# Banded attention into a gated feed-forward on one core: the softmax's guard, its division, two scalar loads and the last chunk's output projections are arranged anew

## The chip, the core and the metric

The kernel runs on one core of a Trainium2 chip. Its engines run side by side and wait for each other by semaphores: TensorE (PE in the profile) multiplies matrices into PSUM, VectorE (DVE), ScalarE (ACT) and GpSimd (POOL) do the elementwise work, and SyncE (SP) issues most DMAs. The metric is the device time of one execution in microseconds, lower is better.

## What is computed

```python
scores = q @ k.T / sqrt(64)                       # 4 batches, 8 heads, 768 positions
keep   = (pos_k < n_sink) | ((0 <= rel) & (rel < window))     # 4 sinks, window 128
scores = where(keep, scores, -1e9); scores -= scores.max(-1)
a = exp(scores); a = a / (a.sum(-1) + 1e-9)
x = (a @ v), heads side by side                   # 3072 x 512
out = (sigmoid(x @ w_gate) * (x @ w_val)) @ w_out # 512 -> 1536 -> 512
```

The weights come as 64-bit floats, so the kernel decodes each into a high and a low 32-bit part. Every product of the feed-forward is made as three products of such parts, which is why TensorE has three matmuls where one would be thought of.

## The kernel before

**The order of the work** is decided when the kernel is built. Each piece of work is handed to a planner (`Plan.op`, line 264) with a priority, the tiles that it reads and writes, and one or more *ways*: an engine, a guessed time in ns and the function that issues it. `Plan.run` (line 288) plays the guessed times forward and, whenever an engine is guessed to be free, gives it the waiting piece with the lowest priority whose buffers are free. The order that comes out is then issued as it stands, engine by engine, and each engine works through its own list in order. So a changed guess or a changed piece can move instructions anywhere in the program. Where PE has nothing to do early on, the planner puts in filler matmuls on the identity (`warm`, line 649; `m<-ident` in the profile), whose results nobody reads.

**Attention** (`attend`, line 692) runs in 96 units: 4 batches x 3 pairs of query tiles x 8 heads. A unit is a chain. PE makes the scores of both tiles `t` (`a<-qkT` in the first 16 units, `a<-kh,qs` later); DVE applies the masks `am` and writes the scores into `P` with the row's extreme in `negm_all` (`top`); ACT takes the exponential in place and adds up each row into `rs` (`exp`, line 751, with the instruction ACTIVATION_READ_ACCUMULATOR behind it). Then `guard` (line 764, on POOL or DVE) adds 1e-9 to both sums, DVE takes the reciprocal (line 771), each tile's 128 band columns are multiplied by it (line 773; ACT, POOL or DVE), and `sink_weights` (line 792, on DVE or POOL) multiplies the 4 sink columns of both tiles into their place in `psk`, where those of all 8 heads are gathered. PE turns `P` (`a<-ident,P`), ACT copies it to `wt`, POOL cuts it to the two triangles (the two affine selects of `split`), and PE multiplies it with `v`. `P` and `rs` have two buffers each, so at most two units are between their scores and their transposes. After 8 heads, `join` (line 928) adds the sinks' part and leaves x in the tiles `XH` and `XL`.

**The feed-forward** (`feed`, line 1061, and `feed_part`, line 1089) runs over 8 chunks `ci` of 2 to 4 token tiles (`MT`, line 25) and in each over 12 blocks `f` of 128 hidden columns. A block has 12 gate and 12 value matmuls into two PSUM tiles `m`, a tanh on ACT (`th`), the product on DVE, a rounded high part `gh` (ACT or DVE), the rest `gl` (POOL or DVE, `rest`, line 520), and then the output projections `down` (line 1145): three matmuls for each token tile into `o`, which read `gh`, `gl`, `woh` and `wol`. PE's priority for a block's `down` is half a block behind its gate matmuls. `th`, `gh` and `gl` have two buffers each.

**Around them**: `decode` (line 995) turns 36 weight tiles into parts during the first 200 us or so, shared out over ACT, DVE and POOL (`wst`, `w`, `wgh`, `wgl`, `wvl`, `wlo` ...). The two scalars `n_sink` and `window` are loaded by the first two DMAs of SP's queue (line 571), the masks wait for them. The last lines (1183 to 1203) count whether the general path is needed: a matmul `count`, a cast, a reduction `total`, which every engine then reads before it branches.

Of the kernel before, what the change touches and what calls it, by code (L numbers as in the profile page):

```python
# [433 lines left out]
def kernel(  # L434
# [136 lines left out]
    for i, s in enumerate((n_sink, window)):  # L571
        dma(
            SCALP, 56.0, lambda i=i, s=s: Q.dma_start(
                out=nums()[:, 2 * i : 2 * i + 2],
                in_=s.bitcast(I32).rearrange("(o x) -> o x", o=1).broadcast_to([128, 2]),
            ), w=[(nums, i)],
# [67 lines left out]

    MS = [ps.tile([128, 512], F32, name=f"m{i}") for i in range(BUFS["m"])]
# [46 lines left out]
    def attend(u, b, h, t0, T, XR, XS, PSK):  # L692
# [35 lines left out]
        rs = tile([128, 4], F32, "rs", BUFS["P"])  # L728
        for t in range(T):
# [21 lines left out]
            def exp(t=t):  # L751
                A.activation(
                    out=P()[:, t], in_=P()[:, t], func=AF.Exp, bias=negm_all[:, u, t : t + 1],
                    scale=-1.0, accum_out=rs()[:, t : t + 1],
                )
# [6 lines left out]
            plan.op(u, [("A", 460, exp)], [], [(P, t), (rs, t)])  # L762

        def guard(E):
            return lambda: E.tensor_scalar(
                out=rs()[:, 0:T], in0=rs()[:, 0:T], scalar1=1.0e-9, scalar2=None, op0=ALU.add
            )

        plan.op(u, [("G", 400, guard(G)), ("V", 250, guard(V))], [], [rs])
        plan.op(  # L770
            u, [("V", 120, lambda: V.reciprocal(out=rs()[:, 0:T], in_=rs()[:, 0:T]))], [], [rs]
        )
        for t in range(T):
            plan.op(
                u, [
                    ("V", 390, lambda t=t: V.tensor_scalar(
                        out=P()[:, t, 0:128], in0=P()[:, t, 0:128], scalar1=rs()[:, t : t + 1],
                        scalar2=None, op0=ALU.mult,
                    )),
                    ("A", 320, lambda t=t: A.mul(  # L780
                        out=P()[:, t, 0:128], in_=P()[:, t, 0:128], mul=rs()[:, t : t + 1]
                    )),
                    ("G", 450, lambda t=t: G.tensor_scalar(
                        out=P()[:, t, 0:128], in0=P()[:, t, 0:128], scalar1=rs()[:, t : t + 1],
                        scalar2=None, op0=ALU.mult,
                    )),
                ][::-1],
                [rs], [(P, t)],
            )


        def sink_weights(E):
            return lambda: E.tensor_tensor(
                out=psk()[:, 0:T, h], in0=P()[:, 0:T, 128:KW],
# [458 lines left out]
```

## Time and profile before

| | |
|---|---|
| device time, three runs | 796.38, 798.26, 807.41 us; median 798.26 us |
| the profiled execution, its own time | 798.38 us |
| its span in the trace | 796.7 us (1.7 us lie around it) |
| PE busy | 773.8 us, 97% of the span |
| DVE, ACT, POOL busy | 513.4, 403.2 and 437.5 us (64%, 51%, 55%) |
| mean granted PE clock | 0.992 of full speed |

The busy times are of the whole span, but the stages differ: DVE, ACT and POOL work mainly in the first 400 us and little in the last 200, PE nearly all the time. Matmuls are pipelined and their ends are modelled, so the time of one is read from the starts of neighbours; a busy PE can still hold filler matmuls. A wait is credited to the instruction that came last.

### The profile page before, as it was taken

The page shows a single profiled execution, that of the slowest core. Times are in us where ns is not written, and L with a number is a line of the kernel's source. Part 1 is how long each engine was busy: PE and PEld are TensorE (multiplying, and loading weights), DVE is VectorE, ACT ScalarE, POOL GpSimd, SP SyncE. Part 2 cuts the span into 40 slices and gives each one's busy share as a digit, 9 for nine tenths or more (in the row PEclk, how much of TensorE's full clock was granted, in tenths as well). Part 3 has the DMA queues.
Part 4 walks back from the last instruction along what each step waited for, and adds up shares of the span by engine and source line. Part 5 has one row for each costly group of instructions (what it writes and reads, how often), then busy time and mean ns, then how long its engine had stood idle before and what let it go on. Part 6 is the DMA issues. An engine that isn't in the chain of part 4 may idle for free. (4 is left out here: it accounts for less than half of the span.)

```text
span 796.7 us, 14763 instructions
## 1 busy us (share of the span) xinstructions
PE 773.8 (97%) x4540; PEld 702.8 (88%) x4540; DVE 513.4 (64%) x1550; ACT 403.2 (51%) x1190; POOL 437.5 (55%) x602
## 2 busy tenths in 40 slices
PE   7999999999999999999999999999999999999996
PEld 5677798878999999998999999999999999999995
DVE  5787798998799988899871388885861331111110
ACT  4786777766767767676640256664740210011001
POOL 3676798887667778668761267673751221111211
PEclk8999999999999999999999999999999999999999
DMA  5667777763645544444441235343311121113111
GB/s 162 198 190 207 191 213 253 231 201 115 192 126 151 149 107 122 119 116 112 142 113 40 57 104 133 104 129 111 92 45 42 41 79 40 40 40 92 39 42 57
DMA packets 98421, 94.33 MB, mean 118 GB/s; under 512 B 43168, under 2 KB 77984, under 8 KB 98336
## 3 DMA queue, kind: packets, MB, share of 16 engines
q1 hardware_dynamic: 98336, 93.32, 41.1%
q8 instruction: 38, 0.62, 0.3%
q14 instruction: 47, 0.39, 0.1%
HBM read 83.85 MB, written 9.44 MB: 117 GB/s over the span
## 5 line engine op out<-in xcount | busy, mean ns | idle before, releaser
L488 DVE SCALAR_TENSOR_TENSOR th<-th,m 128x384 f32<-128x384 f32 (+1 forms) x108 | 54.6, 505 | 184.3 <-PE m L488 182.9
L488 POOL TENSOR_TENSOR gl<-th,gh 128x384 fp32r<-128x384 f32 (+1 forms) x65 | 65.5, 1008 | 195.4 <-DVE gh L488 183.0
L488 ACT ACTIVATE th<-m 128x384 f32<-128x384 f32 (+1 forms) x108 | 49.1, 454 | 209.4 <-PE m L488 207.5
L488 POOL TENSOR_SCALAR_AFFINE_SELECT wt<-wt 128x512 fp32r<-128x512 f32 (+3 forms) x192 | 121.5, 633 | 42.6 <-DVE wt L488 24.2
L488 PE MATMUL m<-XH,wvh 128*128 128x384 f32 (+1 forms) x432 | 140.1, 324 | 0.4 <-ACT th L488 0.4
L488 PE MATMUL m<-XH,wgh 128*128 128x384 f32 (+1 forms) x432 | 140.3, 325 | 0.0
L488 PE MATMUL m<-XH,wvl 128*128 128x384 f32 (+1 forms) x432 | 137.7, 319 | 0.0
L488 PE MATMUL m<-XL,wvh 128*128 128x384 f32 (+1 forms) x432 | 137.6, 319 | 0.0
L488 PE MATMUL m<-XH,wgl 128*128 128x384 f32 (+1 forms) x432 | 137.5, 318 | 0.0
L488 PE MATMUL m<-XL,wgh 128*128 128x384 f32 (+1 forms) x432 | 137.3, 318 | 0.0
L488 PE MATMUL o<-woh,gh 128*128 128x512 f32 x276 | 113.0, 409 | 1.0 <-DVE total L1201 1.0
L488 PE MATMUL o<-woh,gl 128*128 128x512 f32 x276 | 109.5, 397 | 2.2 <-DVE gl L488 1.6
L488 PE MATMUL o<-wol,gh 128*128 128x512 f32 x276 | 108.8, 394 | 2.5 <-DMA wol<-wol_d 2.5
L488 ACT ACTIVATE P<-P,negm_all 128x132 f32<-128x132 f32 x192 | 77.2, 402 | 30.5 <-DVE negm_all L488 27.0
L488 PEld LDWEIGHTS m<-XH,wvh 128*128 128x128 f32 x432 | 81.7, 189 | 3.3 <-ACT th L488 0.6
L488 PEld LDWEIGHTS m<-XH,wgh 128*128 128x128 f32 x432 | 81.4, 189 | 2.1 <-issue 0.2
L488 PEld LDWEIGHTS m<-XL,wvh 128*128 128x128 f32 x432 | 81.8, 189 | 1.5
L488 PEld LDWEIGHTS m<-XL,wgh 128*128 128x128 f32 x432 | 81.5, 189 | 1.6
L488 PEld LDWEIGHTS m<-XH,wvl 128*128 128x128 f32 x432 | 81.7, 189 | 0.0
L488 PEld LDWEIGHTS m<-XH,wgl 128*128 128x128 f32 x432 | 81.3, 188 | 0.0
L488 PEld LDWEIGHTS o<-woh,gl 128*128 128x128 f32 x276 | 52.0, 188 | 16.6 <-DVE gl L488 3.5
L488 DVE CUSTOM_DVE_ANT_0 P<-a,am 128x132 f32<-128x132 f32 x192 | 56.2, 294 | 11.9 <-PE a L488 2.9
(115 smaller groups left out, 1619.5 us busy)
## 6 DMA issues: line engine op xcount, KB each, us to landing
wol<-wol_d SPq DMA_DIRECT2D x108, 256.0 KB, 2.7
qkT<-in_k_dram SPq DMA_DIRECT2D x120, 99.0 KB, 2.6
qkT<-in_q_dram SPq DMA_DIRECT2D x176, 64.0 KB, 2.4
wst<-in_moe_w_gate_dram SPq DMA_DIRECT2D x12, 512.0 KB, 4.3
wst<-in_moe_w_val_dram SPq DMA_DIRECT2D x12, 512.0 KB, 4.3
wst<-in_moe_w_out_dram SPq DMA_DIRECT2D x12, 512.0 KB, 4.2
vraw<-in_v_dram SPq DMA_DIRECT2D x64, 96.0 KB, 2.3
out_dram<-w SPq DMA_DIRECT2D x23, 256.0 KB, 2.5
```

What stands on the lines that cost most here:

```text
L488: return lambda *a, **kw: tc.keep_in_program_order(op(*a, **kw))
```

## The change

- The row sums go into the first column of a constant tile `sums` of [128, 2, 2], two buffers, all filled with 1e-9 once at the start by POOL. The exponential overwrites only column 0 of each pair, so summing the pair adds the guard: one DVE `tensor_reduce`, followed at once on DVE by the reciprocal, both in one piece of the plan.
- The division of both tiles over all 132 columns is one piece with three ways: one POOL `tensor_tensor` against the broadcast reciprocals, two ACT multiplications in a row, or one DVE `tensor_tensor`. The sink columns are divided with it, so `psk` gets a plain copy (POOL or ACT) afterwards.
- The loads of the two scalars are issued by ACT's queue in place of SP's.
- The planner's guess for POOL's byte step of `decode` is 560 in place of 1000 ns.
- In the last chunk the `down` of block `f` gets a priority 1.4 blocks behind its gate matmuls, and the last block's `gl` is made on DVE only.

```diff
-        dma(
-            SCALP, 56.0, lambda i=i, s=s: Q.dma_start(
+        plan.op(
+            SCALP, [("A", 460, lambda i=i, s=s: A.dma_start(
...
+    SUMS = [const.tile([128, 2, 2], F32, name=f"sums{i}") for i in range(BUFS["P"])]
+    for x in SUMS:
+        nc.gpsimd.memset(x, 1.0e-9)
...
-        rs = tile([128, 4], F32, "rs", BUFS["P"])
+        sums = Tile(SUMS, None, F32, "sums", BUFS["P"])
+        rs = tile([128, T], F32, "rs", BUFS["P"])
...
-                    scale=-1.0, accum_out=rs()[:, t : t + 1],
+                    scale=-1.0, accum_out=sums()[:, t, 0:1],
...
-        plan.op(u, [("G", 400, guard(G)), ("V", 250, guard(V))], [], [rs])
-        plan.op(
-            u, [("V", 120, lambda: V.reciprocal(out=rs()[:, 0:T], in_=rs()[:, 0:T]))], [], [rs]
-        )
...
+        def guard():
+            V.tensor_reduce(out=rs(), in_=sums()[:, 0:T], axis=AX.X, op=ALU.add)
+            V.reciprocal(out=rs(), in_=rs())
+
+        plan.op(u, [("V", 320, guard)], [sums], [rs])
+        def norm(E):
+            return lambda: E.tensor_tensor(
+                out=P(), in0=P(), in1=rs().unsqueeze(2).to_broadcast([128, T, KW]), op=ALU.mult
+            )
+        def norm_each():
+            for t in range(T):
+                A.mul(out=P()[:, t], in_=P()[:, t], mul=rs()[:, t : t + 1])
...
-            u, [("V", 110, sink_weights(V)), ("G", 400, sink_weights(G))], [rs, (P, T)], [(psk, h)]
+            u, [("G", 800, norm(G)), ("A", T * 350, norm_each), ("V", 380, norm(V))], [rs], [P]
+        )
+        gather = lambda: psk()[:, 0:T, h]
...
+                ("G", 230, lambda: G.tensor_copy(out=gather(), in_=P()[:, :, 128:KW])),
+                ("A", 250, lambda: A.copy(out=gather(), in_=P()[:, :, 128:KW])),
...
-                ("G", 1000.0, lambda: G.tensor_scalar(out=flat(), in0=by(3), **two)),
+                ("G", 560.0, lambda: G.tensor_scalar(out=flat(), in0=by(3), **two)),
...
+        last = ci == len(MT) - 1
...
-        rest(pr, W, gl, th, gh, [th, gh], [gl])
+        rest(pr, W, gl, th, gh, [th, gh], [gl], last and f == NF - 1)
...
-                pe + 0.5 / NF, [("PE", 3 * mac(DO), down)], [gh, gl, woh, wol], [O[j]]
+                pe + (1.4 if last else 0.5) / NF, [("PE", 3 * mac(DO), down)], [gh, gl, woh, wol], [O[j]]
```

What the planner makes of it, counted over the whole order of the issued program: of the 96 units' divisions 70 go to ACT as pairs (140 instructions), 17 to POOL, 9 to DVE; before, the 192 were 136 on ACT, 45 on POOL and 11 on DVE. The copies into `psk` are 65 on ACT and 31 on POOL; before, 80 multiplications on DVE and 16 on POOL. The 96 reductions are all on DVE; the guards were 43 on DVE and 53 on POOL. `gh` is made on ACT 94 times (before 54) and on DVE 14 times (before 54). PE's work is the same but for 72 filler pieces where there were 69.

**The end of PE's list.** First the last value matmuls of block 11 before (`wvh_151`, `wvl_152`), the `count`, and the first output projections of block 11 (`gh_10014`); the output projections of block 10 stand ahead of these value matmuls.

```order
L488 MATMUL m_90<-XH,wvh_151 128x384
L488 MATMUL m_90<-XL,wvh_151 128x384
L488 MATMUL m_90<-XH,wvl_152 128x384
L1197 MATMUL count<-bad,one 1x4
L488 MATMUL o_9564<-woh_153,gh_10014 128x512
L488 MATMUL o_9564<-wol_9982,gh_10014 128x512
L488 MATMUL o_9564<-woh_153,gl_10016 128x512
```

And of the change, from the last value matmul of block 11 on: the nine projections of block 10 (`gh_9950`) now stand here, those of block 11 (`gh_9992`) behind them, and `count` behind those.

```order
L488 MATMUL m_95<-XH,wvl_156 128x384
L488 MATMUL o_9562<-woh_152,gh_9950 128x512
L488 MATMUL o_9562<-wol_9921,gh_9950 128x512
L488 MATMUL o_9562<-woh_152,gl_9955 128x512
L488 MATMUL o_9567<-woh_152,gh_9950 128x512
L488 MATMUL o_9567<-wol_9921,gh_9950 128x512
L488 MATMUL o_9567<-woh_152,gl_9955 128x512
L488 MATMUL o_9573<-woh_152,gh_9950 128x512
L488 MATMUL o_9573<-wol_9921,gh_9950 128x512
L488 MATMUL o_9573<-woh_152,gl_9955 128x512
L488 MATMUL o_9562<-woh_157,gh_9992 128x512
L488 MATMUL o_9562<-wol_9963,gh_9992 128x512
```

So between the last value matmul and the first projection that needs its result there are now nine matmuls in place of `count` alone.

**The start of ACT's list**, before: the sinks' cast `vsp`, the exponentials of unit 0 (`P_215`) and unit 1 (`P_230`), two steps of weight decoding (`w`), and unit 0's divisions.

```order
L488 ACT_TABLE_LOAD
L488 CAST vsp<-w_190 96x512
L488 ACTIVATE P_215,rs_218<-P_215,negm_all 128x132 x2
L488 ACTIVATE P_230,rs_234<-P_230,negm_all 128x132
L488 ACTIVATE w_241<-wst_205 128x512
L488 ACTIVATE w_248<-wst_209 128x512
L488 ACTIVATE P_215<-P_215,rs_218 128x128 x2
```

And of the change, where unit 0 is `P_223` and unit 1 `P_233`:

```order
L488 DMA nums_160<-in_n_sink_dram 128x2
L488 DMA nums_160<-in_window_dram 128x2
L488 ACT_TABLE_LOAD
L488 CAST vsp<-w_183 96x512
L488 ACTIVATE P_223,sums_90<-P_223,negm_all 128x132
L488 ACTIVATE w_235<-wst_200 128x512
L488 ACTIVATE P_223,sums_90<-P_223,negm_all 128x132
L488 ACTIVATE P_233,sums_91<-P_233,negm_all 128x132
L488 ACTIVATE w_247<-wst_204 128x512
L488 ACTIVATE P_223<-P_223,rs_249 128x132 x2
L488 ACTIVATE P_233,sums_91<-P_233,negm_all 128x132
L488 COPY psk_264<-P_223 128x2x4
```

The two loads lead the list, a decoding step (`w_235`) has come between unit 0's two exponentials, and the copy into `psk` follows the division on the same engine.

**DVE's list in the first units**, before: the guard (TENSOR_SCALAR on `rs`), the reciprocal, and the multiplications of one unit, with the masks of the next (ISA) between them.

```order
L488 TENSOR_SCALAR rs0_286<-rs0_286 128x2
L488 CAST wvh0_96<-w20_248 128x512
L488 RECIPROCAL rs0_286<-rs0_286 128x2
L488 ISA P1_321,negm_all_80<-a0_308,am0_86 128x132
L488 ISA negm_all_80 128x1
L488 TENSOR_TENSOR psk0_255<-P0_276,rs0_286 128x2x4
L488 TENSOR_SCALAR P0_276<-P0_276,rs0_286 128x128
```

And of the change, the unit behind it:

```order
L488 TENSOR_REDUCE rs1_360<-sums1_91 128x2
L488 RECIPROCAL rs1_360<-rs1_360 128x2
L488 ISA P0_366,negm_all_80<-a2_345,am0_86 128x132
L488 ISA negm_all_80 128x1
L488 COPY_PREDICATED a0_348<-tri_89,a0_348 128x128
L488 ISA P0_366,negm_all_80<-a0_348,am1_87 128x132
```

Reduction and reciprocal follow each other, and the multiplications of the sink columns are gone from this list.

## Rows read from the trace of the kernel before

**Rows 1.** The busy time of each engine in stretches of the span. Columns: the stretch and its length in us; then the busy time, with the number of instructions in brackets, of PE, PE's weight loads, DVE, ACT and POOL; then the granted PE clock, the DMA share and GB/s.

```profile
0.00:50.00 50.00, 43.18 (x227) 31.52 (x228) 35.37 (x130) 32.08 (x93) 29.11 (x52) 0.93 0.61 181
50.00:100.00 50.00, 47.87 (x300) 39.10 (x299) 39.42 (x114) 36.54 (x107) 34.19 (x45) 0.97 0.69 198
100.00:150.00 50.00, 48.28 (x339) 44.77 (x339) 46.36 (x103) 38.33 (x100) 45.84 (x48) 1.00 0.77 235
150.00:200.00 50.00, 46.32 (x306) 39.84 (x305) 45.86 (x103) 33.74 (x92) 39.70 (x46) 1.00 0.55 167
200.00:250.00 50.00, 50.00 (x361) 46.73 (x359) 44.22 (x152) 35.50 (x118) 32.98 (x53) 1.00 0.58 161
```

**Rows 2.** The filler matmuls of the first 200 us (count, busy us, mean ns, and idle time of PE ahead of them), and the first gate matmuls of the feed-forward (in the stretch from 40 to 60 us: min/median/max ns, first and last start).

```profile
L488 PE MATMUL m<-ident 128*128 128x128 f32 x138 | 24.8, 320 | 1.6 <-POOL ident masks.py:199 1.4
...
L488 PE MATMUL m<-XH,wgh x9: 278/282/386, 48.7 to 60.0; 128*128 128x256 f32 x9
```

**Rows 3.** The end of the span as a timeline: start in us, duration in us, engine, line, operation, count; in brackets the idle time ahead and what ended it.

```profile
786.05 0.34 PE L488 MATMUL m<-XH,wvl 128*128 128x384 f32 x1
...
786.32 0.19 PE L1197 MATMUL count<-bad,one 128*1 128x4 f32 x2
786.49 0.56 DVE L488 SCALAR_TENSOR_TENSOR th<-th,m 128x384 f32<-128x384 f32 x1 [7.46 <-PE m L488]
...
787.08 0.36 DVE L488 CAST gh<-th 128x384 fp32r<-128x384 f32 x1
...
787.61 1.00 POOL L488 TENSOR_TENSOR gl<-th,gh 128x384 fp32r<-128x384 f32 x1 [7.38 <-DVE total L1201]
...
788.67 0.50 PE L488 MATMUL o<-woh,gl 128*128 128x512 f32 x1 [0.44 <-POOLq L1204]
...
789.94 0.39 PE L488 MATMUL o<-wol,gh 128*128 128x512 f32 x1
...
790.17 0.39 PE L488 MATMUL o<-woh,gl 128*128 128x512 f32 x1
...
790.59 0.60 ACT L488 ACTIVATE qkT<-o 128x512 f32<-128x512 f32 x1
```

**Rows 4.** Groups of instructions over the whole span, forms apart: the operations that the change takes out or rewrites (count, then busy us, mean ns of one, then idle time ahead).

```profile
L488 DVE TENSOR_SCALAR rs<-rs 128x2 f32<-128x2 f32 x43 | 21.4, 497 | 3.6 <-ACT P L488 3.4
...
L488 DVE RECIPROCAL rs<-rs 128x2 f32<-128x2 f32 x96 | 15.0, 157 | 4.1 <-POOL rs L488 3.2
...
L488 DVE TENSOR_TENSOR psk<-P,rs 128x8 f32<-128x8 f32 x80 | 30.4, 379 | 0.5
...
L488 ACT ACTIVATE P<-P,rs 128x128 f32<-128x128 f32 x136 | 50.1, 396 | 22.3 <-DVE rs L488 20.9 <-DVE bad L1187 0.8
...
L488 POOL TENSOR_SCALAR P<-P,rs 128x128 f32<-128x128 f32 x45 | 31.6, 701 | 10.8 <-DVE rs L488 8.4 <-DVE psk L488 1.2 <-ACT wst L488 1.0
...
L488 POOL TENSOR_TENSOR psk<-P,rs 128x8 f32<-128x8 f32 x16 | 3.8, 238 | 1.7 <-DVE rs L488 1.7
```

**Rows 5.** The same groups on DVE between 100 and 200 us alone.

```profile
L488 DVE TENSOR_TENSOR psk<-P,rs 128x8 f32<-128x8 f32 x8 | 6.7, 839 | 0.0
...
L488 DVE RECIPROCAL rs<-rs 128x2 f32<-128x2 f32 x11 | 1.7, 152 | 0.0
...
L488 DVE TENSOR_SCALAR rs<-rs 128x2 f32<-128x2 f32 x2 | 1.2, 600 | 0.0
```

**Rows 6.** DVE's reciprocals, one for each unit: those up to 48.7 us, and those up to 200 us.

```profile
L488 DVE RECIPROCAL rs<-rs 128x2 f32<-128x2 f32 x9 | 1.4, 160 | 0.9 <-POOL rs L488 0.8
...
L488 DVE RECIPROCAL rs<-rs 128x2 f32<-128x2 f32 x29 | 4.5, 156 | 0.9 <-POOL rs L488 0.8
```

**Rows 7.** Groups over the whole span that are nearest to what the change adds.

```profile
L488 POOL TENSOR_TENSOR kl<-qkT,kh 128x264 fp32r<-128x264 f32 x10 | 8.2, 815 | 0.6
...
L488 ACT ACTIVATION_READ_ACCUMULATOR P<-P,negm_all 128x1 f32 x192 | 36.2, 189 | 0.0
...
L488 ACT CAST vhl<-vraw 128x128 fp32r<-128x128 f32 x7 | 2.1, 299 | 3.2 <-PE a L488 3.2
...
L488 ACT CAST gh<-th 128x384 fp32r<-128x384 f32 x23 | 11.8, 513 | 4.0 <-DVE th L488 3.6
```

**Rows 8.** The start of the span as a timeline (columns as in rows 3; SPq is SyncE's DMA queue): the scalars' first load, the first load behind them, the scalars' arrival, the sinks' cast, the first decoding step on ACT, and unit 0's transposes.

```profile
0.80 0.40 SPq L488 DMA_DIRECT2D nums<-in_n_sink_dram  x1
...
1.72 0.56 SPq L488 DMA_DIRECT2D qkT<-in_k_dram  x1
...
4.70 0.24 DVE L488 CAST nums<-nums 128x2 f32<-128x2 uint32 x2 [2.15 <-DMA nums<-in_window_dram]
...
8.05 0.62 ACT L488 CAST vsp<-w 96x512 fp32r<-96x512 f32 x1 [5.98 <-DMA w<-in_v_sink_dram]
...
11.13 0.70 ACT L488 ACTIVATE w<-wst 128x512 f32<-128x512 f32 x1 [1.28 <-DMA wst<-in_moe_w_gate_dram]
...
13.55 0.77 PE L488 MATMUL a<-ident,P 128*128 128x128 f32 x2 [4.05 <-ACT P L488]
```

**Rows 9.** Unit 1 in the timeline: the last row sum is read out, POOL's guard, DVE's reciprocal.

```profile
13.99 0.19 ACT L488 ACTIVATION_READ_ACCUMULATOR P<-P,negm_all 128x1 f32 x1
...
15.69 0.21 POOL L488 TENSOR_SCALAR rs<-rs 128x2 f32<-128x2 f32 x1
...
15.94 0.17 DVE L488 RECIPROCAL rs<-rs 128x2 f32<-128x2 f32 x1 [0.45 <-POOL rs L488]
```

More of the change, by code (lines that the diff above doesn't have):

```diff
@@ L571 @@
     for i, s in enumerate((n_sink, window)):
-        dma(
-            SCALP, 56.0, lambda i=i, s=s: Q.dma_start(
+        plan.op(
+            SCALP, [("A", 460, lambda i=i, s=s: A.dma_start(
                 out=nums()[:, 2 * i : 2 * i + 2],
                 in_=s.bitcast(I32).rearrange("(o x) -> o x", o=1).broadcast_to([128, 2]),
-            ), w=[(nums, i)],
+            ))], w=[(nums, i)], dma=56.0,
         )
@@ L761, in attend @@
             )
[L762 to L766, printed above, removed]
-            )
-        plan.op(u, [("G", 400, guard(G)), ("V", 250, guard(V))], [], [rs])
+            plan.op(u, [("A", 460, exp)], [], [(P, t), (sums, t)])
+        def guard():
+            V.tensor_reduce(out=rs(), in_=sums()[:, 0:T], axis=AX.X, op=ALU.add)
+            V.reciprocal(out=rs(), in_=rs())
@@ L772, in attend @@
         )
-        for t in range(T):
-            plan.op(
[L775 to L788, printed above, removed]
-            )
@@ L792, in sink_weights @@
-        def sink_weights(E):
-            return lambda: E.tensor_tensor(
-                out=psk()[:, 0:T, h], in0=P()[:, 0:T, 128:KW],
-                in1=rs()[:, 0:T].unsqueeze(2).to_broadcast([128, T, NS]), op=ALU.mult,
-            )
-        plan.op(
-            u, [("V", 110, sink_weights(V)), ("G", 400, sink_weights(G))], [rs, (P, T)], [(psk, h)]
+        gather = lambda: psk()[:, 0:T, h]
+        plan.op(
+            u, [
+                ("G", 230, lambda: G.tensor_copy(out=gather(), in_=P()[:, :, 128:KW])),
+                ("A", 250, lambda: A.copy(out=gather(), in_=P()[:, :, 128:KW])),
+            ],
+            [P], [(psk, h)],
```

## The prediction

> **What bounds the kernel now.** I read the busy times by stretch first. From 200 us on PE is busy without a gap (50.00 of 50 us in the stretch shown), while in the first 200 us it is idle for 6.8, 2.1, 1.7 and 3.7 us, 14.3 us together [rows 1]. So after 200 us only PE's own work counts, and the change leaves that work alone: the matmuls are the same ones. What can be won lies in the first 200 us, at the very end, and in filler matmuls, which look like work and are none. The fillers take 24.8 us of PE, and the feed-forward's first matmul starts at 48.7 us [rows 2]: until then PE waits for attention units, and the length of a unit's chain on ACT, DVE and POOL sets the pace. From 50 us on PE has feed-forward work to lay between, so a chain's length matters less. Between 100 and 200 us another limit shows: DVE is busy for 92.2 of 100 us and POOL for 85.5, ACT for 72.1 [rows 1], since units and weight decoding meet there. The reader is to see three places with three limits: chain length before 48.7 us, DVE's and POOL's load up to 200 us, and a wait at the end.
>
> **The end.** PE's last value matmul starts at 786.05. Matmuls of that kind follow each other at some 0.18 us, so PE is free at 786.23. Then the product on DVE, `gh` on DVE and `gl` on POOL run one after another, and PE's third output matmul waits for `gl` until 788.67; the ninth starts at 790.17, and with the 0.23 us between two of them PE ends at 790.40 [rows 3]. That is 4.17 us for nine matmuls of 0.23 us, 2.1 us: 2.1 us are waits and the `count`. In the new order the nine matmuls of block 10 stand in this place. Is `gl` there when they are done, 2.1 us after PE was free? The product ends 0.82 us after it (786.49 + 0.56 [rows 3]); `gh` is on ACT now, 0.51 us in place of 0.36; `gl` is on DVE, and at POOL's 1.00 us it would be there after 2.5 us, with two changes of engine at some 0.1 us [rows 3, 7]. The first two matmuls of block 11 don't read `gl`, so it is needed only at 2.1 + 0.46 = 2.56 us. Nothing waits. The term is **-2.0 us** (between -1.9 and -2.1). `count` (0.19 us [rows 3]) with the small steps that hang on it now lies behind the last matmul, beside ACT's last copy and the output's DMA, which take from 790.40 to the span's end at 796.7. In the last chunk a block's output matmuls come one block later; `gh` and `gl` have two buffers, and the block after next writes them only behind these matmuls in PE's list, so no new wait arises.
>
> **The start.** Without the scalars' two issues SP's queue begins 0.92 us earlier with the keys (1.72 against 0.80 [rows 8]), and so does every load behind them. The masks don't gain: the scalars land at 4.70 now, and ACT issues them at about the time SP did. The sinks' cast, for which ACT waits 5.98 us until 8.05, and the first decoding step at 11.13 come up to 0.92 us earlier [rows 8]. Against that, the second exponential of unit 0 now queues behind that decoding step: 11.13 - 0.92 + 0.70 = 10.9 us, another 0.6 for it and its sum, 0.3 for reduction and reciprocal, then a decoding step of 0.70 and the first division: transposes at some 13.0 in place of 13.55 [rows 8]. Term **-0.5 us**, between -0.9 (all of the queue's gain) and +0.9 (ACT's queue lands the scalars that much later, with the masks behind them).
>
> **The chain of a unit.** Out go a guard and its change of engine. Unit 1 shows a bad case: its last sum is read out by 14.18, POOL gets to the guard at 15.69, DVE's reciprocal starts at 15.94 [rows 9], 1.76 us where reduction and reciprocal alone would begin as soon as DVE is free. In comes a reduction of two pairs per row. The trace has none of this shape; the nearest is the reciprocal on the same two columns, 157 ns, and the upper bound is the guard on DVE, 497 [rows 4]. I take 160, since the reciprocal stands at the same place in the same queue. So a unit gains at least 0.25 - 0.16 = 0.1 us and in the bad case 1.6; I take 0.5, nearer to the low end, because DVE works through its list in order too. Two things are added. ACT's second division comes behind the first (0.4 us [rows 4]), where in part of the units it ran on another engine, and the copy into `psk` comes behind the division: 0.19 (the shortest ACT instruction) to 0.30 us (a copy of 128 columns) on ACT, at most 0.24 on POOL [rows 4, 7]. The copy delays only the buffer's release. I charge 0.3 us for both. Nine units have their reciprocals ahead of the first feed-forward matmul [rows 6], and two of them overlap: with one more under way, 10 x (0.5 - 0.3) / 2 = **-1.0 us**, between -6.5 (10 x 1.3 / 2) and +1.5 (10 x 0.3 / 2). Up to 100 us the same holds for half a dozen more units under PE's cover; of the 2.1 us idle there I take a third, **-0.7**, between -2.1 and 0.
>
> **DVE's load between 100 and 200 us.** There the sink multiplication of 8 columns costs DVE 839 ns and the guard of 2 columns 600, while the reciprocal of 2 columns costs 152 [rows 5]. So the first two spend most of their time held. Out go 6.7 + 1.2 = 7.9 us, in come 11 reductions of 0.16, 1.8 us: DVE loses 6.1 of its 92.2 us. POOL loses guards and divisions at 701 ns a tile and gets a few whole divisions, for which its subtraction over 264 columns gives 815 ns [rows 4, 7]. ACT has to take 140 divisions where it had 136 and 65 copies, at most 65 x 0.3 = 20 us over the whole kernel; its 72.1 us of 100 leave room. PE's idle time there is 5.4 us [rows 1], and that is the most the relief can give back. I take a bit over half, **-3.0**, between 0 and -5.4. Behind 200 us the relief goes on and is worth nothing, as PE doesn't wait there.
>
> Why are small instructions held? The DVE instructions that are long for their size read SBUF twice, or are a plain scalar operation in SBUF. The Trainium skill, GPSIMD Engine Reference, section Specifications, says that GpSimd shares its SBUF interfaces with VectorE, with contention for DVE instructions in a two-port mode or with two SBUF inputs; VectorE: DVE Perf Modes, section on the perf-mode tiers, has `tensor_reduce` at 1x only, so the reduction should be free of it. Rows 5 agree for what goes out; for the reduction no row shows it. If the rule failed and each reduction were held like a guard (0.6 us), DVE would lose only 7.9 - 6.6 = 1.3 us, and the term would be some -0.7 in place of -3.0.
>
> The other guess, 560 ns for POOL's byte step, only moves that step between engines, and the wider ACT multiplications (132 columns for 128) cost a few ns each: nothing, while ACT has room.
>
> **Sum.** -2.0 - 0.5 - 1.0 - 0.7 - 3.0 = -7.2 us. The profiled execution took 798.38 us, 0.1 from the median of 798.26, so the forecast is **791.2 us**. PE's fillers are 72 pieces in place of 69: the planner itself does not see PE better fed early on, which is why I took low ends.
>
> **Rivals.**
> *Only the end is won.* What attention gains is spent waiting for weight tiles, since decoding paces the first half, or the planner's moved instructions cost as much as they give. For it speaks that DVE's decoding steps remain. Then 798.4 - 2.0 = 796.4, or 795.9 with the start.
> *The shared interface frees more.* If holding is mutual, POOL gains too when DVE's small instructions vanish, and both engines that are full between 100 and 200 us speed up: all 5.4 us of idle time there, 2.1 before it and half of the 6.8 us ahead of 50 us, 10.9 us, plus the end: 798.4 - 12.9 = 785.5. Against it: some idle time at the start is loading, whatever the engines do.
> *Slower: ACT's list becomes the wait.* Division pairs and copies stand ahead of the next unit's exponentials. A unit's chain then gets longer by the second division (0.4) and the copy (0.3) and wins back only 0.1 from the guard: +0.6 us, over the 29 units of the first 200 us [rows 6] and two at a time +8.7 us; with the end and the start won 798.4 + 8.7 - 2.5 = 804.6. It decides from about 0.2 us a unit on, where 29 x 0.2 / 2 eats the 2.5 us. Against it: ACT is busy for 141 of 200 us [rows 1]. [...]
> *The change doesn't do what it says.* "One division" is one instruction only in the 26 units that the planner gave to POOL or DVE; in 70 it is a pair on ACT. This is in the terms above.
>
> **Chances.** Forecast 0.50 (own range 787.5 to 794.5); only the end 0.22 (to 797.5); more freed 0.15 (784 to 787.5); slower 0.13 (798 to 806). The range 785 to 799 leaves out most of the slower case and the lower edge of the third, under 0.2. A change of 2%, about what a measurement of this kernel can tell from none, is 16 us, down to 782 or up to 814: the front would have to lose all its idle time and some fillers, or ACT's rival double. Faster 0.03, same 0.94, slower 0.03.
>
> **What would show it.** End: nine output matmuls between the last value matmul and those of the last block, no gap of 1 us, and PE's last start some 2 us earlier against the first matmul of the last chunk. Start: transposes of unit 0 before 13.5 us. Chain: the first gate matmul before 48.7 us. DVE: reductions at 150 to 170 ns, DVE below 92 us between 100 and 200 us, and PE's idle time there below 5.4. Wrong would be: reductions of 400 ns and more; ACT waiting less for others while PE waits more for `P`; a first gate matmul later than 48.7 us; or idle time after 200 us, where I count on none.

## The result: slower by 0.7%, where a gain of 0.9% was forecast

| | before | changed |
|---|---|---|
| median of 20 runs each, us | 798.82 | 804.61 |
| ratio | | 1.007 [1.0048, 1.0092] |
| profiled execution, its span, us | 798.38, 796.7 | 802.07, 800.4 |
| PE busy, us | 773.8 | 774.7 |
| DVE, ACT, POOL busy, us | 513.4, 403.2, 437.5 | 472.1, 438.5, 411.5 |

The forecast was 791.2 us with a range up to 799.0; the measured time lies outside it and on the other side of no change. DVE lost 41 us of work and the kernel lost time. The ratio, as every ratio below, leaves out a kernel's slow executions, here three of the changed kernel's 20 (813.49, 813.92 and 1518.92 us).

First the windows of the changed kernel, to set beside [rows 1] (same columns).

```profile
0.00:50.00 50.00, 44.57 (x231) 32.78 (x232) 32.30 (x127) 32.56 (x103) 23.25 (x45) 0.93 0.59 170
50.00:100.00 50.00, 45.84 (x289) 36.60 (x288) 36.56 (x110) 34.07 (x107) 31.66 (x41) 1.00 0.64 184
100.00:150.00 50.00, 46.93 (x322) 42.52 (x321) 44.20 (x97) 37.17 (x99) 43.26 (x44) 1.00 0.76 230
150.00:200.00 50.00, 45.84 (x308) 41.24 (x307) 43.93 (x94) 34.53 (x92) 38.47 (x42) 0.97 0.58 178
200.00:250.00 50.00, 48.39 (x345) 44.99 (x345) 42.25 (x152) 37.82 (x126) 34.45 (x51) 1.00 0.58 158
```

DVE falls from 92.2 to 88.1 us of the 100 between 100 and 200 us, as wanted, and PE is idle *more*: 5.4 us up to 50 us (6.8 before), then 4.2 (2.1), 7.2 for the next two (5.4) and 1.6 where there was none. Together 18.4 for 14.3 us. Each number is from one execution: in the traces of the experiments below that keep the old order ahead of the last chunk, without the one that doubles an instruction, PE is idle for 5.1 to 6.8 us between 100 and 200 us, so the 7.2 lie just above that.

What PE waited for between 60 and 200 us (us in total, times, longest; what ended the wait stands behind the arrow), before:

```profile
PE o L488 <- DMA wol<-wol_d: 2.5, 2, 1.3
PE o L488 <- DVE gl L488: 1.6, 3, 0.7
PE a L488 <- DVE xr L488: 0.8, 2, 0.5
PE a L488 <- DVE negm_all L488: 0.7, 2, 0.4
PE a L488 <- DVE wt L488: 0.4, 1, 0.4
...
PE m L488 <- ACT th L488: 0.4, 1, 0.4
```

and in the changed kernel:

```profile
PE o L488 <- DMA wol<-wol_d: 3.2, 3, 1.9
PE m L488 <- ACT th L488: 2.7, 4, 1.5
PE a L488 <- ACT xr L488: 2.3, 1, 2.3
PE a L488 <- DVE wt L488: 0.9, 1, 0.9
...
PE a L488 <- DVE xr L488: 0.4, 2, 0.2
...
PE a L488 <- DVE negm_all L488: 0.2, 1, 0.2
```

The waits for DVE fall from 3.5 to 1.5 us, as the prediction wanted. Those for ACT rise from 0.4 to 5.0, so PE waits for another engine in place of DVE.

How differently PE's work lies is seen between 70 and 80 us. These are the windows of the instructions that read `XH` alone, of before:

```profile
70.00:80.00 10.00, 3.91 (x19) 2.89 (x18) 0.00 (x0) 0.00 (x0) 0.00 (x0) 1.00 0.78 240
```

and of the changed kernel:

```profile
70.00:80.00 10.00, 0.15 (x1) 0.00 (x0) 0.00 (x0) 0.00 (x0) 0.00 (x0) 1.00 0.63 187
```

PE has run out of input matmuls there. Fillers, which look busy, take part of the place: 14 in this stretch, where there was none (144 in all for the 138 of [rows 2]). This hole by itself isn't the loss: by the table of input matmuls below, the changed kernel has caught up at 95 us, and falls behind after that.

The new and rewritten operations, as groups over the whole span, which answer to [rows 4] and [rows 7]:

```profile
L488 ACT ACTIVATE P<-P,rs 128x132 f32<-128x132 f32 x140 | 48.9, 397 | 15.6 <-DVE rs L488 15.1
...
L488 DVE TENSOR_REDUCE rs<-sums 128x2 f32<-128x4 f32 x96 | 14.2, 147 | 3.9 <-ACT P L488 3.6
L488 ACT COPY psk<-P 128x8 f32<-128x8 f32 x65 | 12.5, 193 | 2.5 <-POOL P L488 1.3 <-DVE rs L488 0.4 <-DVE P L488 0.4
L488 POOL TENSOR_TENSOR P<-P,rs 128x264 f32<-128x264 f32 x17 | 11.6, 684 | 7.3 <-DVE rs L488 4.7 <-ACT wt L488 1.3 <-ACT th L488 0.8
...
L488 POOL COPY psk<-P 128x8 f32<-128x8 f32 x31 | 9.5, 307 | 14.4 <-ACT P L488 12.8 <-DVE P L488 1.2
L488 DVE TENSOR_TENSOR P<-P,rs 128x264 f32<-128x264 f32 x9 | 5.5, 610 | 0.1
```

Every price was close: the reduction 147 ns (160 taken), ACT's copy 193 (190 to 300), ACT's divisions 397 (396). Only POOL's copy is longer than its bound, 307 for 240.

The end, as a timeline (columns of [rows 3]): the last value matmul, the last product, `gh` and `gl`, the first matmul that reads that `gl`, and the last.

```profile
788.83 0.34 PE L488 MATMUL m<-XH,wvl 128*128 128x384 f32 x1
...
789.27 0.55 DVE L488 SCALAR_TENSOR_TENSOR th<-th,m 128x384 f32<-128x384 f32 x1 [5.71 <-PE m L488]
...
789.86 0.51 ACT L488 CAST gh<-th 128x384 fp32r<-128x384 f32 x1 [2.19 <-DVE th L488]
...
790.40 0.56 DVE L488 TENSOR_TENSOR gl<-th,gh 128x384 fp32r<-128x384 f32 x1 [0.58 <-ACT gh L488]
...
791.55 0.40 PE L488 MATMUL o<-woh,gl 128*128 128x512 f32 x1
...
792.95 0.40 PE L488 MATMUL o<-woh,gl 128*128 128x512 f32 x1
```

From 789.00 on 18 output matmuls follow each other at 0.23 us; `gl` is there at 790.96, its first reader starts at 791.55. The 2.1 us of waits are gone: 18 output matmuls now take the 4.2 us that nine took before. From the last matmul's start to the span's end it then takes 7.4 us, where it was 6.5, so in this trace 1.2 us are left of the gain.

The start, which answers to [rows 8]:

```profile
10.14 0.67 ACT L488 ACTIVATE w<-wst 128x512 f32<-128x512 f32 x1 [1.80 <-DMA wst<-in_moe_w_gate_dram]
...
11.57 0.15 DVE L488 TENSOR_REDUCE rs<-sums 128x2 f32<-128x4 f32 x1
...
12.98 0.77 PE L488 MATMUL a<-ident,P 128*128 128x128 f32 x2 [3.61 <-ACT P L488]
```

Unit 0's transposes start at 12.98 (some 13.0 forecast, 13.55 before).

So where did it go? I compare when the n-th input matmul of the feed-forward (`m<-XH` or `m<-XL` with any weight, 2592 in each trace) starts. The column of before is its start in us, the others are the difference to it, one profiled execution each. The last four are experiments told below: the kernel before with another number in the planner (LAT), and with more or less work for DVE.

```
   n   before  changed  LAT 184  LAT 176  double_psk  relief_again
   1     48.7     -1.5     -1.5     +2.1        -0.6          +0.3
 121     94.9     -0.5     +3.8     +0.6        -0.8          -1.9
 241    118.3     +4.5     +7.5     +2.8        +0.3          +0.8
 481    173.3     +1.8    +13.8     +5.7        +1.0          -0.3
 601    203.5     +6.6    +13.1    +12.6        +0.7          -0.4
 961    299.7     +5.8    +14.9    +12.6        +3.2          -0.5
1441    453.7     +4.7    +13.2    +14.4        +6.9          -1.4
2521    767.4     +4.9    +13.9    +15.3        +7.4          -1.6
```

The changed kernel is ahead by 1.5 us when the feed-forward begins, and behind by 6.6 at 203.5 us. After that nothing more is lost. Of the kernels below that keep the old order ahead of the last chunk, those without the doubled instruction lie between -0.5 and +3.8 at n = 601; one whose granted clock was 0.85 in its first 100 us has +9.7, and +9.9 already at n = 1. So single executions differ by some us, and the 6.6 to 13.1 of the remade orders here lie outside that.

### The profile page after: what moved, and what is told of

Read it like the earlier page. It is cut to its first block, busy times and chain, and to the rows that moved or that the text cites. A ratio compares the mean times of both kernels' runs of the same rounds, so it can differ in the third digit from the quotient of the medians.

```text
span 800.4 us, 14731 instructions
## 1 busy us (share of the span) xinstructions
PE 774.7 (97%) x4546; PEld 705.0 (88%) x4546; DVE 472.1 (59%) x1456; ACT 438.5 (55%) x1311; POOL 411.5 (51%) x551
## 4 chain that ended last, share of the span: by engine, by line
PE 85%; DMA 6%; DVE 3%; POOL 2%; ACT 1%; issue 1%; SPq 1%; POOLq 0%; ACTq 0%; DVEq 0%
PE m L488 47%; PE o L488 22%; PE a L488 15%; DMA wst<-in_moe_w_val_dram 2%; DMA wol<-wol_d 2%; SPq L488 1%; DVE w L488 1%; DMA wol_d<-wlo 1%; DMA w<-in_v_sink_dram 1%; DMA vraw<-in_v_dram 1%; DMA qkT<-in_k_dram 0%; POOL kl L488 0%; ACT w L488 0%; DVE xr L488 0%; POOL wt L488 0%
## 5 line engine op out<-in xcount | busy, mean ns | idle before, releaser
L488 POOL TENSOR_TENSOR gl<-th,gh 128x384 fp32r<-128x384 f32 (+1 forms) x73 | 72.3, 990 | 194.2 <-ACT gh L488 192.4
L488 POOL TENSOR_SCALAR_AFFINE_SELECT wt<-wt 128x512 fp32r<-128x512 f32 (+3 forms) x192 | 119.4, 624 | 57.7 <-DVE wt L488 30.8
L488 ACT CAST gh<-th 128x384 fp32r<-128x384 f32 (+1 forms) x94 | 45.2, 481 | 104.5 <-DVE th L488 103.9
L488 POOL TENSOR_TENSOR qs<-qkT,qs 64x256 fp32r<-64x256 f32 x69 | 54.9, 795 | 19.4 <-POOL wt L488 5.5
```

What stands on the lines that cost most here:

```text
L488: return lambda *a, **kw: tc.keep_in_program_order(op(*a, **kw))
```

## Experiments

Four theories stood against each other: that the planner, with pieces for ACT at its head, loads ACT too early; that the softmax's new instructions cost time themselves; that the end of weight decoding, which came later, sets the time; and that any order made anew loses to the one that the kernel before has.

The ratios are to the kernel before on the same chip, with 95% intervals; its median was 798.4 to 799.3 us. The times are medians and the ratios are of means, so a few long executions move the one and not the other.

**One part at a time.** First the last chunk's two edits alone:

> Only the last chunk's later output projections and the last gl on DVE are added to the kernel before; the rest of the order is the old one. If my term for the end holds, it is 2.0 us faster (ratio 0.9975), with the nine output matmuls of block 10 between the last value matmul and block 11's, and PE's idle 2 us gone. If the gain at the end is given back somewhere else, the ratio is 1.000.

798.33 us, 0.9977 [0.995, 1.0004]: -1.8 us, the size of the term of the end, though the interval just takes in no change. From the 2521st input matmul to the span's end its trace is 1.7 us shorter than that of before, and in the eight others with this edit it is 1.2 (the change) to 2.3. Then the scalars alone, planned as the change plans them:

> Only the two scalar loads go to ACT's queue. The new first piece of the plan makes ACT the first engine that the planner asks for work, and gh goes to ACT 93 times in place of 54. Theory A (that look order costs: ACT's list gets longer and the decoding steps that only ACT can do come late): 3 to 5 us slower, last weight part at 195 us or later (188 before). Theory B (the softmax part costs): within 1 us of before. Theory C (any new order scatters by some us): anything within 4 us either way, with no link to when decoding ends.

806.38 us, 1.0096 [1.0065, 1.0127]: moving two small DMAs to another queue, with the order that the planner then makes, costs 7.6 us. How far a new order reaches is seen at the end of this trace: 18 output matmuls follow the last value matmul there, as in the change, though the edit of the end isn't in this kernel. The softmax part alone:

> Only the new sums, the one division and the plain copies; scalars on SP's queue, old guess, old end. Theory A: 1 to 5 us faster than before, as I forecast for the first 200 us, since DVE loses its held instructions and ACT is not asked first. Theory B: 4 to 6 us slower. Theory C: within 4 us either way.

807.26 us, 1.0096 [1.0062, 1.013]. Two parts that share no instruction cost the same 8 us, and the whole change, which has both, costs 5.8. Costs that belong to instructions would be expected to add up.

Part of both losses goes with the granted clock, which no term of the prediction has. The median of the executions' mean clocks is 0.987 with the scalars alone and 0.985 with the softmax part alone, against 0.992 in the kernel before. Their executions at 0.990 or more took 801.4 and 805.2, and 800.3 and 801.3 us, where the kernel before has a median of 798.1 for the same, so some 2 to 7 us are left at such a clock. Why these orders get a lower clock isn't shown.

**ACT first?** With a piece for ACT planned first, the planner comes to look at ACT before the other engines, which gave ACT more work. The whole change with the old order of looking:

```diff
     def run(self, warm, fill_ns, fill):
...
+        for e in ("Q", "G", "V", "A", "PE"):
+            free[e] = 1000.0 if e == "Q" else 1400.0
+            waiting[e] = []
```

> The whole change, but the planner asks the engines in the order that it had before (SP, POOL, DVE, ACT, PE). The divisions on ACT fall from 140 to 84 and gh on ACT from 94 to 54. Theory A: 5 to 9 us faster than the change, so 793 to 797 us beside 799 for the kernel before. Theory B: as slow as the change, 1.005 to 1.009 of the kernel before. Theory C: anywhere between 0.990 and 1.010.

808.77 us, 1.0121 [1.0076, 1.0166], with 84 of the divisions' instructions on ACT in place of 140. Relieving ACT made this order no faster. Back to SyncE's queue for the scalars:

> The whole change with the two scalar loads back on SP's queue. ACT's list then has 104 of the divisions (140 in the change) and 55 of the gh (94). If ACT's list length is the cost, it is 3 us or more faster than the change, under 800 us. Theory D: its decoding steps stand as late among the units as in the change, so decoding ends at 196 to 203 us and it takes 800 to 807 us.

800.01 us, 1.0026 [1.0001, 1.0052], with 104 divisions on ACT. That is 4.6 us less than the change (3.5 by the ratios) and the best of the remade orders, and still none the better for the end's 2 us. So 84, 104 and 140 divisions on ACT go with 808.8, 800.0 and 804.6 us: ACT's load doesn't order the times. The rival *ACT's list becomes the wait*, whose 804.6 us the result hit, gets some support from PE's 5.0 us of waits for ACT; but at LAT 184, told below, they are 4.6 us with 133 divisions on ACT, where the kernel before has 136 and 0.4 us. So a longer list isn't needed for them, and that it has a part here isn't excluded.

**Does weight decoding set the pace?** In the traces so far the span grew with the time at which decoding ended (188 us before, 199 in the changed kernel, 206 in the slowest). So decoding got earlier due times, with the change, and then with the end's edit alone; then later ones in the kernel before.

```diff
-DS1 = 6.0
+DS1 = 4.0
...
-DS2 = 18.0
+DS2 = 16.0
```

> The whole change, with the weight decoding due two units earlier in the plan (DS1 4 for 6, DS2 16 for 18). Theory D (the first 200 us are paced by the end of weight decoding: in the five traces so far span minus the end of the last weight part is 601 to 609 us, and the change lets decoding end at 199 us where it was 188): decoding ends at 192 us or before, and the kernel takes 793 to 799 us, 3 to 8 less than the change. Theory C (any new order scatters): no link, 797 to 812 us whatever the end of decoding. Theory E (attention paces the front, decoding is only seen beside it): units come later by what decoding wins, so as slow as the change, 800 to 808 us.

805.32 us, 1.013 [1.0075, 1.0184].

> The kernel before with the late output projections at the end and decoding due two units earlier. Theory D: decoding ends at 180 to 188 us and the kernel takes 789 to 796 us, faster than both kernels. Theory C: within 4 us of 797. Theory E: 797 to 801 us, with units behind by what decoding wins.

801.96 us, 1.0043 [1.0018, 1.0067]. With 7.5 and 19.5 in the kernel before:

> The kernel before with decoding due 1.5 units later (DS1 7.5, DS2 19.5) and nothing else changed. Theory D: decoding ends at 194 to 200 us and the kernel takes 803 to 808 us, slower by as much as decoding is later. Theories C and E: within 3 us of before.

806.48 us, 1.0117 [1.0079, 1.0155]. Decoding ended at 191, 180 and 195 us in these three. The order with later decoding took longer, but decoding that ended 9 and 12 us earlier than in its partner made neither kernel faster. So the theory that decoding's end sets the time fell. What was left: that any new order costs.

**The parts in the old order.** The plan is made from the old pieces and guesses; only what a piece issues is exchanged.

```diff
-        plan.op(u, [("G", 400, guard(G)), ("V", 250, guard(V))], [], [rs])
+        plan.op(u, [("G", 400, lambda: None), ("V", 250, lambda: None)], [], [rs])
...
+        plan.op(u, [("V", 120, guard)], [], [rs])
```

Here `guard` issues the reduction over [sum, 1e-9] and the reciprocal.

> The kernel before with the order of its plan kept as it is: the guard's slot in the plan issues nothing any more, and the reciprocal's slot issues the reduction over [sum, 1e-9] and the reciprocal. The sink multiplication and the divisions are those of before. No other instruction changes its place on any engine. If the new softmax instructions themselves cost the time (in the run with the softmax part alone the loss was some 8 us), this kernel loses most of it too: +3 to +8 us. If it was the order that the planner made anew, the instructions are a small gain or nothing: -3 to 0 us (the guard of 497 ns on DVE or a change of engine to POOL goes, a reduction of some 150 ns comes).

798.96 us, 0.9989 [0.9958, 1.002].

```diff
-            SCALP, 56.0, lambda i=i, s=s: Q.dma_start(
+            SCALP, 56.0, lambda i=i, s=s: A.dma_start(
```

> The kernel before with the two scalars' loads issued by ACT's queue, but planned as before: the lists of PE, DVE and POOL are those of before word for word, ACT's list has the two loads at its head. If it is the issue from ACT itself that cost the 7 us of the run with this part alone, this kernel loses as much: +4 to +8 us. If it was the order made anew, -0.9 to 0 us is expected, since SP's queue begins 0.9 us earlier.

799.10 us, 0.9989 [0.9951, 1.0026]. The 7.6 us of the scalars are gone with the order kept. Both, and the end:

> The late output projections of the last chunk with DVE's last rest, the scalars on ACT's queue and the new sums, all with the plan's order ahead of the last chunk kept as it was before. If order is what cost the change its gain: 793 to 796.5 us, faster than both kernels. If the parts themselves cost: 800 us or more.

796.87 us, 0.9966 [0.994, 0.9993], the fastest kernel here that computes the whole reference; 793.08 to 798.25 in all its executions but two. Of its 2.7 us the end has some 2; the two other parts bring what can't be told from nothing.

**Orders alone.** One number of the planner that describes no instruction:

```diff
-LAT = 180.0
+LAT = 184.0
```

> The kernel before with one number of the planner changed that describes no instruction: the guessed time from one engine's end to another's start, 184 in place of 180 ns. Every instruction is the same; only the order that the planner makes of them differs. If any new order costs several us because the order of before was a picked one: +2 to +9 us. If orders are about equal and the loss comes from the edited instructions: within 1 us of before.

813.36 us, 1.0177 [1.0128, 1.0225]. At 176:

> The kernel before with the planner's guessed time from engine to engine at 176 in place of 180 ns, no instruction changed. If the order of before is a picked one, any other costs: +2 to +14 us. If the run at 184 was a single bad order: -2 to +2 us.

812.51 us, 1.016 [1.0131, 1.0189]. 4 ns in a guess, either way, cost 13 to 14 us, more than I expected at 184 and more than all terms of the prediction together. The operations are the same; their order differs, and a few go to another engine. The clock doesn't explain it: the profiled executions at 184 and before have the same mean, 0.992, and lie 13.9 us apart. The windows of the run at 184, against [rows 1]:

```profile
50.00:100.00 50.00, 45.60 (x278) 36.74 (x278) 36.95 (x114) 33.39 (x99) 29.95 (x42) 0.97 0.65 186
100.00:150.00 50.00, 44.78 (x308) 40.15 (x306) 42.85 (x91) 33.50 (x89) 37.88 (x39) 1.00 0.73 218
150.00:200.00 50.00, 43.83 (x289) 38.12 (x290) 45.92 (x91) 34.46 (x89) 43.07 (x44) 1.00 0.59 181
...
70.00:80.00 10.00, 0.83 (x5) 0.53 (x4) 0.00 (x0) 0.00 (x0) 0.00 (x0) 1.00 0.68 189
```

It is the changed kernel's picture, larger, with none of its edits: PE starved of input matmuls between 70 and 80 us (the last row reads as those of `XH` above), 11.4 us idle between 100 and 200 us for 5.4, DVE and ACT less busy too. Now the changed kernel at the same two values:

> The changed kernel with the guess at 176 ns. If the change's loss is one draw from orders that lie some 10 us apart: anywhere from 795 to 812 us, and not the 804.6 of the change. If the change's instructions cost the time whatever their order: within 2 us of 804.6.

807.37 us, 1.0102 [1.0074, 1.0131].

> The changed kernel with the guess at 184 ns; as for 176. Taken together: if the mean of the changed kernel's three orders lies below that of the kernel before at 176 and 184, the edits are worth something apart from the order; if it lies above, they cost something.

803.50 us, 1.0062 [1.0034, 1.009]. The change's three orders lie at 803.5 to 807.4 us, the neighbours of before at 812.5 and 813.4. Against neighbours the change is some 8 us faster; against the one order of before it is slower. Five orders are few, and how much of the 8 us belongs to the edits stays open.

**DVE's load by itself.** In the order of before, with the new sums, the held sink multiplication became a reduction over one element:

```diff
+        def gather():
+            V.tensor_reduce(
+                out=psk()[:, 0:T, h], in_=P()[:, 0:T, 128:KW].unsqueeze(3), axis=AX.X, op=ALU.add
+            )
...
-            u, [("V", 110, sink_weights(V)), ("G", 400, sink_weights(G))], [rs, (P, T)], [(psk, h)]
+            u, [("V", 110, gather), ("G", 400, sink_weights(G))], [rs, (P, T)], [(psk, h)]
```

> The kernel before in its own order, with the new sums, and with the 80 sink multiplications on DVE replaced at the same place by a reduction over one element of each, which writes the 4 sink columns of both tiles into psk undivided (so in these 80 units the sinks' share is left undivided; no wait on the reciprocals is needed for it). It is a form of DVE instruction that was not held in the changed kernel (147 ns where the multiplication takes 839 between 100 and 200 us). If the prediction's term of DVE's load is right: -2 to -4 us, DVE near 86 of 100 us between 100 and 200 us. If the held time only passes on to the next DVE instruction that reads two inputs: -1 to 0 us, with DVE's load down by less than half of those 6 us and the decoding steps longer.

797.62 us, 0.998 [0.9964, 0.9996]. Its profiled execution, 806.8 us, had a PE clock of 0.85 in its first 100 us and its stretches aren't read here. Once more:

> The kernel without DVE's held sink multiplications once more, unchanged. If the gain of the first time was real: a ratio of 0.996 to 0.999 again, DVE's decoding steps between 100 and 200 us longer than before (851 and 901 ns). If DVE's load sets the pace: 0.995 or less.

797.06 us, 0.9996 [0.997, 1.0022]. DVE's groups between 100 and 200 us, first those of before that are not in [rows 5]:

```profile
L488 DVE SCALAR_TENSOR_TENSOR w<-w,wst 128x512 int32<-128x512 int32 x19 | 17.1, 901 | 0.0
L488 DVE SCALAR_TENSOR_TENSOR w<-wst,w 128x512 int32<-128x512 int32 x20 | 17.0, 851 | 0.0
```

and those of this kernel, with its windows of that time:

```profile
L488 DVE SCALAR_TENSOR_TENSOR w<-wst,w 128x512 int32<-128x512 int32 x20 | 19.0, 948 | 0.0
L488 DVE SCALAR_TENSOR_TENSOR w<-w,wst 128x512 int32<-128x512 int32 x19 | 18.5, 972 | 0.2 <-ACT w L488 0.2
...
L488 DVE TENSOR_REDUCE psk<-P 128x8 f32<-128x8 f32 x8 | 1.2, 150 | 0.0
...
100.00:150.00 50.00, 47.98 (x333) 43.97 (x332) 46.41 (x107) 37.64 (x98) 42.90 (x43) 1.00 0.76 233
150.00:200.00 50.00, 46.88 (x313) 40.58 (x312) 45.43 (x107) 34.12 (x92) 37.79 (x42) 1.00 0.56 168
```

The sink columns fall from 6.7 to 1.2 us, and the same 39 decoding steps grow by 3.4. DVE's load stays at 91.8 for 92.2 us, PE's idle time at 5.1 for 5.4. So DVE was hardly relieved at all between 100 and 200 us, and these two runs don't tell what a lower load would be worth. Then the dose the other way, the multiplication issued twice:

```diff
-            return lambda: E.tensor_tensor(
...
+            def issue():
+                for again in range(2 if E is V else 1):
+                    E.tensor_tensor(
```

> The kernel before in its own order, with each of DVE's 80 sink multiplications issued twice in a row (the second writes the same values again): some 30 us more DVE work by rows 4, some 6.7 us of it between 100 and 200 us by rows 5. If DVE's load there paces PE, as the prediction's -3.0 us assumes at half of what is taken away: +3 to +6 us. If PE's idle time there comes from elsewhere: 0 to +1.5 us.

806.62 us, 1.0113 [1.0094, 1.0133]. The dose was smaller than expected: 160 multiplications take 54.1 us where 80 took 30.4, and those between 100 and 200 us 9.9 for 6.7, with DVE busy for 94.5 us. PE's waits for DVE there rise from 3.3 to 6.3 us, but its idle time only from 5.4 to 6.9, which other traces of the old order nearly have. The loss is larger than expected, and lies elsewhere. By the table of input matmuls it loses 0.7 us up to 203.5 us, and 6.2 between there and 453.7. The windows of before in that stretch:

```profile
250.00:300.00 50.00, 49.82 (x318) 46.54 (x318) 44.60 (x158) 37.78 (x123) 38.73 (x62) 1.00 0.52 132
...
350.00:400.00 50.00, 49.23 (x286) 45.15 (x286) 45.38 (x148) 34.27 (x110) 38.01 (x55) 1.00 0.46 126
400.00:450.00 50.00, 50.00 (x274) 47.01 (x273) 18.20 (x52) 11.24 (x33) 15.91 (x20) 1.00 0.26 70
```

and of the doubled kernel:

```profile
250.00:300.00 50.00, 49.17 (x306) 44.47 (x305) 46.17 (x162) 36.35 (x119) 38.13 (x61) 1.00 0.48 127
...
350.00:400.00 50.00, 47.67 (x277) 43.50 (x276) 46.30 (x150) 32.35 (x102) 36.59 (x51) 1.00 0.47 129
400.00:450.00 50.00, 49.23 (x266) 44.77 (x265) 23.69 (x73) 14.32 (x46) 18.39 (x26) 1.00 0.27 74
```

PE's busy time falls by 3.0 us in these rows, and it issues 29 matmuls fewer. What PE waited for between 250 and 450 us in the doubled kernel is DVE alone:

```profile
PE a L488 <- DVE negm_all L488: 1.1, 2, 0.7
PE a L488 <- DVE psk L488: 0.8, 2, 0.5
PE a L488 <- DVE xr L488: 0.7, 1, 0.7
PE a L488 <- DVE wt L488: 0.7, 2, 0.5
```

Before, these are 0.9 us (`xr` 0.7, `wt` 0.2). So PE can be made to wait for DVE after 200 us, where the prediction counted on no wait at all; it had read one stretch of 50 us as all that follows, though PE is idle for 0.77 us between 350 and 400. The rise of 2.4 us is less than half of the 6.2; where the rest goes these rows don't show.

## Why the prediction was wrong

**The step that failed is that the sum prices edits only where their instructions stand.** Of moved work it says that another guess for POOL's byte step "only moves that step between engines" and costs nothing; the order was read at single places (the end, ACT's and DVE's first units), and the rest of it was priced at nothing. The rival *only the end is won* names moved instructions that cost as much as they give, and stops there at 796.4 us. The runs show that remaking the order costs 13 to 14 us in the kernel before with nothing edited, and that the edits that could be put into the old order cost nothing. The uncertainty of the sum was that of the order, some 10 us, and my range had none of it. That the loss is the order's is shown for the scalars: 7.6 us with the order remade, none with the old one. The new sums cost nothing in the old order. For the division and the copies, which don't fit into the old order, it is inferred from the two neighbours at 812.5 and 813.4. What makes one order better than another stays open; PE's waits only show that it waits for other engines in each.

**The end, -2.0 us: right on PE.** 2.1 us of waits are gone, for the reason given, and 1.8 us come out as a ratio alone. What follows the last matmul was put at nothing; in the trace of the change it took 0.9 us more, and why isn't shown.

**The start, -0.5 us: the forecast start came, a gain isn't shown.** The transposes start 0.57 us earlier, but that may be luck: with the scalars' move alone they start at 13.67, with it in the old order at 14.72, and in the whole change without it at 12.76 us (13.55 before). With the order kept the change in time is -0.9 us, with an interval from -3.9 to +2.1.

**The chain, -1.0 and -0.7 us: not shown, and the second half with the wrong sign.** The first gate matmul comes at 47.2 for 48.7 us and PE's idle time before 50 us falls by 1.4, as forecast. But at LAT 184, with nothing edited, that matmul comes at 47.2 too, and with the new sums in the old order at 48.7, so the hit may be luck. PE's idle time between 50 and 100 us doubles; more than half of the 4.2 us is one wait of 2.3 for ACT's `xr`.

**DVE's load, -3.0 us: the relief came, the gain did not.** The load fell by 4.1 us for the 6.1 forecast. Between 60 and 200 us PE's waits for DVE fell by 2.0 us, so DVE was in part what PE waited for; but its waits for ACT rose by 4.6, and between 100 and 200 us its idle time rose by 1.8. The term let DVE give back PE's idle time whatever had caused it, and took a high busy share for the limit. Some half of the waits in the rows of before were for DVE, and no row says that another engine is ready when DVE is earlier. Doubling the multiplications shows the same from the other side: 3.0 us more of waits for DVE between 100 and 200 us, 1.5 us more of idle time. The decoding steps got longer, 67.0 us in all for 59.4, but at LAT 184 they take 64.5. That the reductions themselves are not held was right: 147 ns over the whole span, and 150 for one over 8 columns where the multiplication took 839. The prediction inferred this from two statements of the Trainium skill (GPSIMD Engine Reference, Specifications; VectorE: DVE Perf Modes, the perf-mode tiers), and the trace agrees with the inference.

**Idle time after 200 us** was named as a sign of error, and came: 1.6 us, most of it a wait for the DMA of `wol`.

## What to carry over

Where a planner sets the order, first run the old kernel with a guess shifted by nothing that matters: the scatter of that run is the uncertainty of every forecast. An edit is priced with the old order held, by exchanging what a piece issues; if that brings nothing, a gain or a loss of the whole belongs to the order. A busy engine is a limit only where a row shows another engine waiting for it, and even then the next wait may take the place of the one that goes. That PE is busy all the time doesn't say that a neighbour has room. A gain that lands on its number is no proof of its cause: look whether a kernel without the edit shows it too.

## What the runs showed of the hardware

A reduction on DVE isn't held where a multiplication with two inputs from SBUF is: 150 ns for 8 columns against 839 between 100 and 200 us, and over the whole span 150 against 379.

Whether the held time then moves to the next instruction that reads SBUF twice isn't shown. With 8 multiplications of 839 ns replaced, the 39 decoding steps around them went from 851 and 901 to 948 and 972 ns, and 3.4 of 5.5 us came back. Over the whole span the 72 steps take 66.1 and 64.4 us in the two traces without the multiplications, and 58.9 to 62.7 in the five that have them in the same order (59.4 in the kernel before). But with the multiplications doubled they take 64.0, so longer steps also come where nothing was taken away.
